# A third pair of token chunks by Strassen's products in an attention and feed-forward kernel, with sums and small scalings moved between engines

## The chip, the cores and the metric

The kernel runs on one core of a Trainium2 chip. The core has TensorE for matrix products (PE in the profile, with PEld for its weight loads), VectorE (DVE), ScalarE (ACT), GpSimd (POOL) and SyncE (SP), whose queue issues nearly all DMA transfers here. The metric is the device time of one execution in microseconds, the median of several executions.

## The reference, cut to what matters

```python
# attention over pooled keys, q, k, v: [8 batches, 8 heads, 576 tokens, 64]
k_p = k.reshape(B, H, 72, 8, D).mean(axis=3)
v_p = v.reshape(B, H, 72, 8, D).mean(axis=3)
scores = scale * np.matmul(q, k_p.transpose(0, 1, 3, 2))
scores = scores - np.max(scores, axis=-1, keepdims=True)
attn = np.exp(scores)
attn = attn / (np.sum(attn, axis=-1, keepdims=True) + 1e-09)
x = np.matmul(attn, v_p)            # then [4608 tokens, 512]
# feed-forward, w1, w2: [512, 1024], w3: [1024, 1024], w_out: [1024, 512]
a = x @ w1
b = x @ w2
out = ((a * b) @ w3) @ w_out
```

## The kernel before

The 4608 tokens are 12 chunks of 384 columns. `w3 @ w_out` is formed once at the start (`w_mm`, L1048), as eight blocks `W[j]`. Every large product is made of three TensorE passes over a high and a low part of each operand (`PASSES`), in float32r.

**A plain chunk** m (`range(NP)`, L1363) has eight units j. A unit is twelve matmuls of 384 columns for a (`a_mm`), twelve for b (`b_mm`), both at L785, and nine matmuls of 512 columns that add `(a*b)` times `W[j]` to three PSUM accumulators (`out_mm`, L817, L833). Between them ScalarE copies a (`a_post`), VectorE multiplies (`b_post`), ScalarE rounds to the high part (`g_hi`, L810) and VectorE subtracts for the low part (`g_lo`, L815).

**A pair** M takes two chunks at once (L1392): per unit, seven block products of six matmuls of 384 columns each (`prod`, L951, L962) replace the 48 matmuls that the two chunks would need for a and b. The inputs are sums and differences of blocks of x (`x_sum1` to `x_plo`, tiles `X`) and of the weights (`mix`, L878, written to DRAM as `ws` and read back through a ring of eleven tiles of 256 KB, `load_u`, L942). The results of the products meet in PSUM banks a, b and c: `s1_copy`, `s5_copy`, `s2_copy` on ScalarE, `c11`, `c12`, `c22`, `g_first`, `g_second` on VectorE. The seventh product adds to bank a, and so needs `c22` (L987) to have read what the sixth left there; the sixth needs `s2_copy` (L976) likewise. The out products of the pair's first chunk are spread between the products of the next unit (`out_some`, L848), so that most units have some of them ahead of the seventh product; those of its second chunk follow the eight units (`out_mm` again). Before the change `NP` is 8: chunks 0 to 7 are plain, and chunks 8 and 9, 10 and 11 are pairs 4 and 5.

**Attention** for later chunks runs between these products: scores on TensorE (`s_mm`, L533), softmax on VectorE and ScalarE (`soft1` to `soft2`), transposes by VectorE and through DRAM (`te_turn`, `te_out`, `te_in`), and the product with v (`av_mm`, L737). K and V are summed over groups of eight either by one VectorE reduction (`pool_red`, L467) or by three adds on GpSimd (`pool_tree`, L470). `SOFT_ACT` names the tiles of tokens whose exponentials also give the sums on ScalarE, tile by tile of heads.

**The order of work** on every engine is one list. Each function is put into it with a slot number by `at(kind, k, fn, ...)` (three slots to a unit of a plain chunk), the number is corrected by hand in a table `SHIFT`, and the list is sorted. `M0` is the slot at which chunk 0 begins, `M1 = M0 + 24*NP` that of the first pair. The same list sets the order of SP's queue, which works in order: a transfer that waits for its buffer holds up all behind it.

Of the kernel before, what the change touches and what calls it, by code (L numbers as in the profile page):

```python
# [19 lines left out]
def kernel(  # L20
# [40 lines left out]
    SOFT_ACT = [(0, 0), (0, 1), (1, 0), (1, 1), (1, 2), (1, 3), (2, 1), (2, 2), (3, 1), (3, 2), (4, 1), (4, 2),  # L61
        (4, 3), (5, 0), (5, 1), (5, 2), (6, 0), (6, 1), (6, 2), (7, 1), (7, 3), (8, 1), (8, 2), (9, 1), (9, 2),
        (10, 1), (10, 2), (10, 3), (11, 1), (11, 2)]
    HALF = [(0, 2), (2, 0), (3, 0), (4, 0), (5, 0), (6, 0), (7, 0), (8, 0), (9, 0), (10, 0), (10, 2), (11, 0)]
# [997 lines left out]
    def W_lo(i):  # L1062
# [10 lines left out]
        "g_first": {(4, 6): 0.5, (5, 6): 0.5},
        "g_hi": {(0, 0): 0.75, (0, 1): 0.5, (0, 2): 0.25, (0, 4): 0.5, (0, 6): 0.5, (10, 0): -0.25, (10, 3):
            -0.5, (2, 3): 0.75, (9, 0): 0.5},
        "g_lo": {(0, 0): 0.25, (0, 1): 0.75, (0, 2): 2.5, (0, 4): 0.25, (0, 7): 1.75, (10, 0): 0.75, (10,
# [11 lines left out]
        "load_k": {(0, 0): 3.25, (0, 2): 1},  # L1088
        "load_q": {(11, (3,)): -0.25, (5, (3,)): 0.75, (7, (3,)): 0.75, (9, (3,)): 0.75},
        "load_qt": {(0, 0): -0.5, (0, 1): -0.25, (0, 2): 2},  # L1090
        "load_v": {(0, 0): -0.75, (0, 1): -2},
# [3 lines left out]
            -22.75, (3,): -31, (4,): -10, (5,): -22, (8,): -0.25},  # L1095
        "load_wo": {(0,): -44, (1,): -30, (2,): -5},
        "mix": {(7, 0): -0.75},
        "mix_hi": {(3, 1): 0.5, (5, 0): -0.5, (5, 1): -0.5, (7, 0): -0.5, (7, 1): -0.5},
        "mix_lo": {(3, 1): 0.5, (6, 0): 0.75, (6, 1): 0.75},
        "mix_load": {(1, 0): -0.25},  # L1100
        "mix_out": {(5, 0): 1, (5, 1): 1},
        "plain_out": {(5, 1): 0.75, (7, 1): 0.75},
        "prep_k": {(0, 0): 3.5, (0, 1): 1.25, (1, 0): 0.5, (1, 1): 0.5, (1, 2): -0.75},
        "prep_v": {(1, 1): 5.25},
# [386 lines left out]
```

## Time and profile before

| | |
|---|---|
| median of 3 runs | 743.82 us (743.68 to 746.69) |
| profiled execution, device time | 744.73 us |
| its span, first to last instruction | 742.8 us |
| outside its span | 1.93 us |
| PE busy | 730.5 us, 98% |
| DVE, ACT, POOL busy | 469.8, 352.8, 174.9 us |

The span is the part of the profiled execution that the trace shows; the 1.93 us before and after it belong to the time as well. Busy times are unions of an engine's instructions. Durations of single matmuls overlap, so a matmul's cost is read from the distance between starts.

### The profile page before, as it was taken

The page shows a single profiled execution, that of the slowest core. Times are in us where ns is not written, and L with a number is a line of the kernel's source. Part 1 is how long each engine was busy: PE and PEld are TensorE (multiplying, and loading weights), DVE is VectorE, ACT ScalarE, POOL GpSimd, SP SyncE. Part 2 cuts the span into 40 slices and gives each one's busy share as a digit, 9 for nine tenths or more (in the row PEclk, how much of TensorE's full clock was granted, in tenths as well). Part 3 has the DMA queues.
Part 4 walks back from the last instruction along what each step waited for, and adds up shares of the span by engine and source line. Part 5 has one row for each costly group of instructions (what it writes and reads, how often), then busy time and mean ns, then how long its engine had stood idle before and what let it go on. Part 6 is the DMA issues. An engine that isn't in the chain of part 4 may idle for free.

```text
span 742.8 us, 12190 instructions
## 1 busy us (share of the span) xinstructions
PE 730.5 (98%) x4088; PEld 681.1 (92%) x4088; DVE 469.8 (63%) x875; ACT 352.8 (47%) x1059; POOL 174.9 (24%) x228
## 2 busy tenths in 40 slices
PE   7999999999999999999999999999999999999997
PEld 6888999999999999999999999999989999899996
DVE  4788877665675845664658658566885586633342
ACT  6888986442442634434433434353454344422222
POOL 2244384033431531004503312033042000000000
PEclk9999999999999999999999999999999999999999
DMA  8989935187386465486656463826498859176611
GB/s 288 360 258 307 310 125 125 49 227 191 106 212 155 147 161 153 129 198 181 176 125 185 130 169 97 175 81 155 115 333 241 237 169 301 64 211 197 198 56 42
DMA packets 177741, 132.60 MB, mean 179 GB/s; under 512 B 78352, under 2 KB 145104, under 8 KB 177680
## 3 DMA queue, kind: packets, MB, share of 16 engines
q1 hardware_dynamic: 177536, 131.70, 62.4%
q8 instruction: 32, 0.52, 0.3%
q14 instruction: 29, 0.24, 0.1%
q10 hardware_dynamic: 144, 0.13, 0.1%
HBM read 94.63 MB, written 37.16 MB: 177 GB/s over the span
## 4 chain that ended last, share of the span: by engine, by line
PE 95%; DMA 3%; DVE 1%; SPq 0%; issue 0%; ACT 0%; DVEq 0%; ACTq 0%
PE o L833 22%; PE a L785 18%; PE b L785 18%; PE a L962 8%; PE att L533 5%; PE att L737 5%; PE o L1054 4%; PE o L848 4%; PE att L962 4%; PE b L962 2%; DMA raw<-in_moe_w_dram 1%; PE b L1054 1%; PE a L1054 1%; DMA D<-T 1%; DMA PTl<-D 1%; PE att L238 1%
## 5 line engine op out<-in xcount | busy, mean ns | idle before, releaser
L833 PE MATMUL o<-Wc,gh 128*128 128x512 f32 (+1 forms) x480 | 149.3, 392 | 0.0
L785 PE MATMUL b<-xT,hl 128*128 128x384 f32 x768 | 145.7, 339 | 0.0
L785 PE MATMUL a<-xT,hl 128*128 128x384 f32 x768 | 145.6, 338 | 0.0
L785 PEld LDWEIGHTS a<-xT,hl 128*128 128x128 f32 x768 | 133.4, 188 | 2.9
L785 PEld LDWEIGHTS b<-xT,hl 128*128 128x128 f32 x768 | 132.8, 188 | 0.0
L810 ACT CAST gh<-a 128x384 fp32r<-128x384 f32 x80 | 41.0, 513 | 126.5 <-DVE a L805 103.3
L833 PEld LDWEIGHTS o<-Wc,gh 128*128 128x128 f32 x480 | 87.4, 188 | 13.9 <-DVE ob L863 0.2
L833 PE MATMUL o<-Wc,gl 128*128 128x512 f32 (+1 forms) x240 | 93.1, 388 | 0.2 <-DVE gl L815 0.2
L571 ACT ACTIVATE E<-att,mx 128x72 f32<-128x72 f32 (+1 forms) x240 | 73.5, 324 | 28.2 <-DVE mx L549 26.5
L962 PE MATMUL a<-X,ring 128*128 128x384 f32 x384 | 77.6, 337 | 2.7 <-DVE tmp L987 1.7
L962 PEld LDWEIGHTS a<-X,ring 128*128 128x128 f32 x384 | 67.7, 188 | 6.5 <-DVE tmp L987 2.3
L805 DVE TENSOR_TENSOR a<-b,a 128x384 f32<-128x384 f32 x64 | 35.1, 549 | 50.3 <-PE b L785 48.5
L795 ACT COPY a<-a 128x384 f32<-128x384 f32 x64 | 30.8, 482 | 73.6 <-PE a L785 73.4
L471 POOL TENSOR_TENSOR st<-st 128x512 f32<-128x512 f32 (+2 forms) x29 | 38.6, 1333 | 113.0 <-DMA st<-in_v_dram 63.2
L833 PEld LDWEIGHTS o<-Wc,gl 128*128 128x128 f32 x240 | 45.0, 188 | 10.6 <-DVE gl L815 1.1
L815 DVE TENSOR_TENSOR gl<-a,gh 128x384 fp32r<-128x384 f32 x80 | 47.1, 589 | 6.9 <-ACT gh L810 6.5
L882 POOL TENSOR_TENSOR mix<-mix 128x256 f32<-128x256 f32 x16 | 13.1, 819 | 161.2 <-DMA mix<-wr 132.1
L571 ACT ACTIVATION_READ_ACCUMULATOR E<-att,mx 128x1 f32 (+1 forms) x240 | 50.1, 209 | 0.0
L533 PE MATMUL att<-kbd,qT 128*128 128x144 f32 (+1 forms) x320 | 49.9, 286 | 0.0
L533 PEld LDWEIGHTS att<-kbd,qT 128*128 128x128 f32 (+1 forms) x320 | 45.8, 179 | 1.7
L549 DVE TENSOR_REDUCE mx<-att 128x4 f32<-128x288 f32 (+1 forms) x80 | 35.3, 446 | 16.3 <-PE att L533 16.1
L1054 PE MATMUL o<-hl 128*128 128x512 f32 x144 | 38.8, 401 | 0.0
(158 smaller groups left out, 1167.7 us busy)
## 6 DMA issues: line engine op xcount, KB each, us to landing
ring<-ws SPq DMA_DIRECT2D x112, 256.0 KB
raw<-in_moe_w_dram SPq DMA_DIRECT2D x32, 512.0 KB
out_dram<-ob SPq DMA_DIRECT2D x35, 256.0 KB
st<-in_v_dram SPq DMA_DIRECT2D x16, 512.0 KB
ws<-mix SPq DMA_DIRECT2D x32, 256.0 KB
st<-in_k_dram SPq DMA_DIRECT2D x24, 288.0 KB
qs<-in_q_dram SPq DMA_DIRECT2D x112, 48.0 KB
D<-T SPq DMA_DIRECT2D x7, 768.0 KB
```

The costliest lines, as they stand in the source:

```text
L471: eng.tensor_tensor(out=t[:, :, 0:4], in0=t[:, :, 0:4], in1=t[:, :, 4:8], op=ALU.add)
L533: nc.tensor.matmul(out=ps[:nt, 2 * KP * j:2 * KP * (j + 1)], lhsT=qT[n][:, pr, off:off + nt], rhs=kbd[b % 2][:, pr], start=True, stop=True,)
L549: nc.vector.tensor_reduce(out=mx[:nt, hs], in_=sv, axis=AX.X, op=ALU.min)
L571: nc.scalar.activation(out=E[:nt, h], in_=sv[:, i], func=AF.Exp, scale=-1.0, bias=mx[:nt, h:h + 1], accum_out=sm[:nt, h:h + 1])
L737: nc.tensor.matmul(out=Tp[n, pr, "x"][:, off:off + cnt], lhsT=parts[x][0], rhs=parts[x][1], start=x == 0, stop=x == 3)
L785: nc.tensor.matmul(out=o, lhsT=w12[j, w][sw][:, kt * P:(kt + 1) * P], rhs=x[sx][:, kt], start=(i == 0), stop=(i == 3 * NK - 1))
L805: nc.vector.tensor_tensor(out=g, in0=ps[:, :CH], in1=g, op=ALU.mult)
L810: nc.scalar.copy(out=gh, in_=g)
L815: eng.tensor_tensor(out=gl, in0=g, in1=f(gh), op=ALU.subtract)
L833: nc.tensor.matmul(out=o, lhsT=(gh, gl)[sg][:, c], rhs=W[j][sw][:, d], start=(j == 0 and i == 0), stop=(j == NJ - 1 and i == 2))
L962: nc.tensor.matmul(out=o, lhsT=w[:, kt, sw], rhs=x[sx][:, kt], start=first and n == 0, stop=n == 5, skip_group_check=True)
L1054: nc.tensor.matmul(out=wacc[h][it], lhsT=w3t[s][sa][:, it * P:(it + 1) * P], rhs=wo[j][sb], start=(j == 0 and i == 0), stop=(j == NJ - 1 a ...
```

## The change

`NP` goes from 8 to 6: chunks 6 and 7 become pair 3. K and V sums on VectorE are made by the three adds instead of one reduction, and 16 of them (14 of K, 2 of V) instead of 19 are on VectorE; five of the sixteen weight mixes go from GpSimd to VectorE. For the 29 tiles in `SOFT_ACT` (30 before) the sum is scaled on ScalarE. The last unit's out product of the chunk or pair ahead of a pair is put later, so that it stands between the pair's sixth and seventh product, and the copies of that chunk's result go with it. The mixes and the plain parts of the weights are written to DRAM earlier; q of chunk 7 is staged in two of the four K/V staging tiles; many slot numbers change.

```diff
-    NP = 8
+    NP = 6
...
-    MIX_DVE = []
+    MIX_DVE = [(2, 0), (2, 1), (5, 1), (7, 0), (7, 1)]
...
-    K_RED = [(2, 2), (2, 3), (3, 1), (3, 2), (3, 3), (4, 0), (4, 1), (4, 2), (4, 3), (5, 1), (5, 2), (5, 3), (6,
-        1), (6, 3), (7, 1), (7, 2), (7, 3)]
-    V_RED = [(5, 0), (5, 1)]
+    K_RED = [(2, 2), (2, 3), (3, 1), (3, 2), (3, 3), (4, 1), (4, 2), (5, 0), (5, 1), (5, 3), (6, 0), (6, 2), (7,
+        1), (7, 2)]
+    V_RED = [(3, 0), (7, 1)]
...
     def q_stage(n, pr):
-        if False:
+        if n == NP + 1:
             if pr % 2 == 0:
                 stage["q", n, pr // 2] = st_tile([P, 2 * CH])
...
             if (b, i) in K_RED:
-                pool_red(t[:KP], km[b][:KP, i])
+                pool_tree(t[:KP], km[b][:KP, i], nc.vector)
...
-    def pool_red(t, dst):
-        nc.vector.tensor_reduce(out=dst, in_=t.rearrange("k a e d -> k a d e"), axis=AX.X, op=ALU.add)
-
...
-        (pool_red if (b, hf) in V_RED else pool_tree)(stage.pop(("v", b, hf)), vm[b][:, 2 * hf:2 * hf + 2])
+        eng = nc.vector if (b, hf) in V_RED else nc.gpsimd
+        pool_tree(stage.pop(("v", b, hf)), vm[b][:, 2 * hf:2 * hf + 2], eng)
...
-        nc.vector.tensor_scalar(
-            out=sm[:nt], in0=sm[:nt], scalar1=1e-9, scalar2=float(POOL), op0=ALU.add, op1=ALU.mult)
+        if (n, t) in SOFT_ACT:
+            nc.scalar.activation(out=sm[:nt], in_=sm[:nt], func=AF.Copy, scale=float(POOL), bias=POOL * 1e-9)
+        else:
+            nc.vector.tensor_scalar(
+                out=sm[:nt], in0=sm[:nt], scalar1=1e-9, scalar2=float(POOL), op0=ALU.add, op1=ALU.mult)
...
-            at("M", k + 5, out_mm, m, j)
+            at("M", k + 5 + 1.2 * ((m, j) == (NP - 1, NJ - 1)), out_mm, m, j)
         for t in range(3):
-            at("P", m0 + 3 * NJ + 3, out_post, m, t)
+            at("P", m0 + 3 * NJ + 3 + 2 * (m == NP - 1), out_post, m, t)
...
-        k = M0 + 30 + 24 * (u // 3) + 6 * (u % 3)
+        k = M0 + 6 + 24 * ((u + 2) // 4) + 5 * ((u + 2) % 4)
...
-        at("L", M0 + PLAIN + 8 * u, plain_out, j, kt)
+        at("L", M0 + PLAIN + 6 * u, plain_out, j, kt)
...
-            at("M", k + 1 + j, out_mm, 2 * M + 1, j)
+            at("M", k + 1 + j + 3.2 * (j == NJ - 1 and M < NCH // 2 - 1), out_mm, 2 * M + 1, j)
         if M < NCH // 2 - 1:
             for t in range(3):
-                at("P", k + 1 + NJ, out_post, 2 * M + 1, t)
+                at("P", k + 5 + NJ, out_post, 2 * M + 1, t)
...
+        if n == NP + 1:
+            k = BASE[n] = k - 3
...
-                k2 = x + 2 + 2 * kt
+                k2 = x + 2 - (n == NP + 1) + 2 * kt
...
-            plan_q(n, *((k - 3.25, 0.5, k - 1.5, 0.5) if n == NP + 1 else (k - 8, 1, k - 4, 1)))
+            plan_q(n, *((k - 9, 0.5, k - 4.5, 0.5) if n == NP + 1 else (k - 8, 1, k - 4, 1)))
...
-            plan_v(b, k + 1, k + 3, k + 6, k + 9, k + 10)
+            plan_v(b, *(k + x - 8 * (b == 4) for x in (1, 3, 6, 9, 10)))
```

The rest of the diff is new entries of the lists `SOFT_ACT` and `HALF` and of `SHIFT`: `c11` one slot later in nearly every unit of a pair, `load_u` one slot later in all, `g_lo` mostly later, and the first loads of `w3` (3 and 4) and `w_out` (0) earlier.

## Rows read from the trace of the kernel before

**Rows 1.** The page: engines' busy time, share of the span and instructions.

```profile
PE 730.5 (98%) x4088; PEld 681.1 (92%) x4088; DVE 469.8 (63%) x875; ACT 352.8 (47%) x1059; POOL 174.9 (24%) x228
```

**Rows 2.** Stretches: start, plain chunks, pair 4, pair 5; busy times, clock, DMA.

```profile
0.00:76.60 76.60, 71.15 (x395) 60.50 (x396) 56.91 (x109) 62.48 (x147) 27.66 (x39) 1.00 0.97 306
76.60:536.80 460.20, 460.02 (x2604) 434.85 (x2603) 303.29 (x557) 218.12 (x711) 134.38 (x174) 1.00 0.58 153
536.80:645.90 109.10, 107.17 (x590) 99.50 (x589) 76.53 (x151) 49.85 (x157) 12.82 (x16) 1.00 0.74 224
645.90:742.80 96.90, 92.19 (x505) 86.28 (x503) 33.09 (x60) 22.36 (x45) 0.00 (x0) 0.99 0.48 147
```

**Rows 3.** PE's waits before 76.6 us for weights: us in total, times, longest.

```profile
PE att L238 <- DVE Wc L186: 1.4, 1, 1.4
...
PE att L236 <- DVE Wc L186: 0.9, 1, 0.9
```

**Rows 4.** Timeline of PE in a plain unit: start, length, work.

```profile
504.16 2.24 PE L785 MATMUL b<-xT,hl 128*128 128x384 f32 x12
506.24 0.62 PE L833 MATMUL o<-Wc,gh 128*128 128x512 f32 x2
...
508.29 2.24 PE L785 MATMUL a<-xT,hl 128*128 128x384 f32 x12
```

**Rows 5.** Timeline of PE in pair 5: two products in a row.

```profile
646.98 1.20 PE L962 MATMUL a<-X,ring 128*128 128x384 f32 x6
648.02 1.20 PE L962 MATMUL att<-X,ring 128*128 128x384 f32 x6
```

**Rows 6.** Timeline of PE: a sixth product, then its three waits inside the pairs.

```profile
545.72 1.31 PE L962 MATMUL a<-X,ring 128*128 128x384 f32 x6
547.98 1.31 PE L962 MATMUL a<-X,ring 128*128 128x384 f32 x6 [0.95 <-DVE tmp L987]
...
576.71 1.31 PE L962 MATMUL a<-X,ring 128*128 128x384 f32 x6 [0.96 <-ACT tmp L976]
...
653.08 1.31 PE L962 MATMUL a<-X,ring 128*128 128x384 f32 x6 [0.74 <-DVE tmp L987]
```

**Rows 7.** Groups by form, whole span: sums of K by reduction, adds of these sizes.

```profile
L468 DVE TENSOR_REDUCE km<-st 72x128 f32<-72x1024 f32 x17 | 34.0, 1998 | 0.6 <-DMA st<-in_k_dram 0.5
...
L418 DVE TENSOR_TENSOR st<-st 128x512 f32<-128x512 f32 x2 | 1.4, 693 | 0.9 <-DMA st<-in_k_dram 0.9
...
L422 DVE TENSOR_TENSOR km<-st 64x128 f32<-64x128 f32 x4 | 1.1, 287 | 0.2
...
L419 DVE TENSOR_TENSOR st<-st 128x256 f32<-128x256 f32 x2 | 0.8, 425 | 0.1
```

**Rows 8.** Source line of the scaled sum: nanoseconds least, median, most.

```profile
L591 DVE TENSOR_SCALAR sm<-sm x40: 124/168/1277, 52.0 to 609.1; 128x8 f32<-128x8 f32 x24, 96x8 f32<-96x8 f32 x16
```

**Rows 9.** Source line of g_lo in pair 4, then pair 5: nanoseconds.

```profile
L815 DVE TENSOR_TENSOR gl<-a,gh x9: 544/558/1396, 536.8 to 622.6; 128x384 fp32r<-128x384 f32 x9
...
L815 DVE TENSOR_TENSOR gl<-a,gh x8: 558/558/559, 653.2 to 717.7; 128x384 fp32r<-128x384 f32 x8
```

**Rows 10.** Timeline at pair 4's start: VectorE, then GpSimd.

```profile
548.04 1.40 DVE L815 TENSOR_TENSOR gl<-a,gh 128x384 fp32r<-128x384 f32 x1
...
546.31 0.74 POOL L472 TENSOR_TENSOR st<-st 128x256 f32<-128x256 f32 x1
547.12 0.65 POOL L473 TENSOR_TENSOR vm<-st 128x128 f32<-128x128 f32 x1
547.74 1.28 POOL L471 TENSOR_TENSOR st<-st 128x512 f32<-128x512 f32 x1
```

**Rows 11.** What SP's queue waited for in pair 4: the longest.

```profile
SPq L866 <- ACT ob L865: 16.6, 1, 16.6
```

**Rows 12.** The page: DMA issues by kind, count and size.

```profile
ring<-ws SPq DMA_DIRECT2D x112, 256.0 KB
...
st<-in_k_dram SPq DMA_DIRECT2D x24, 288.0 KB
```

More of the change, by code (lines that the diff above doesn't have):

```diff
@@ L59 @@
     SLOTS, SLOTS1 = 11, 3
[L61 to L64, printed above, removed]
+    SOFT_ACT = [(0, 0), (0, 1), (1, 0), (1, 1), (1, 2), (1, 3), (2, 1), (2, 2), (3, 1), (3, 2), (4, 1), (5, 0),
+        (5, 2), (6, 0), (6, 1), (6, 2), (7, 0), (7, 1), (7, 2), (7, 3), (8, 1), (8, 2), (9, 1), (9, 2), (10, 1),
+        (10, 2), (10, 3), (11, 1), (11, 2)]
+    HALF = [(0, 2), (2, 0), (3, 0), (4, 0), (5, 1), (5, 2), (6, 0), (7, 0), (7, 3), (8, 0), (9, 0), (10, 0),
+        (10, 2), (11, 0)]
     LO12_POOL = [(0, 1), (2, 1), (3, 0), (3, 1), (4, 0), (4, 1), (5, 1), (7, 1)]
@@ L1068 @@
         "W_lo": {(1,): 0.25, (2,): 0.5, (3,): 12, (5,): 2.25, (6,): 2.25, (7,): 2.75},
+        "a_post": {(5, 0): 0.25, (5, 1): 0.25, (5, 2): 0.25, (5, 3): 0.25, (5, 4): 0.25, (5, 5): 0.25, (5,
+            6): 0.25, (5, 7): 0.25},
         "av_lo": {(0, 0): 0.25, (0, 1): 0.75, (0, 2): 0.75, (0, 3): 1, (1, 0): 0.5, (8, 3): 3.5},
-        "av_mm": {(0, 3): 0.5, (1, 0): 0.5, (8, 3): 3.75},
+        "av_mm": {(0, 3): 0.5, (1, 0): 0.5, (11, 2): -1, (5, 2): -1, (7, 2): -1, (8, 3): 3.75, (9, 2): -1},
         "av_post": {(0, 0): 0.25, (0, 3): 0.5, (1, 0): 0.5, (8, 3): 3},
         "b_post": {(0, 4): 0.25},
[L1073 to L1076, printed above, removed]
[7 rows of a table removed]
[4 rows of a table added]
+        "g_first": {(3, 0): 0.25, (3, 2): 0.5, (3, 6): 0.5, (4, 0): 0.25, (4, 6): 0.5, (5, 6): 0.5},
+        "g_hi": {(0, 0): 0.75, (0, 1): 0.5, (0, 2): 0.25, (0, 4): 0.5, (0, 6): 0.5, (10, 1): 0.25, (10, 2):
[7 rows of a table added]
+        "g_lo": {(0, 0): 0.25, (0, 1): 0.75, (0, 2): 2.5, (0, 4): 0.25, (0, 7): 1.75, (10, 0): 1.25, (10,
[12 rows of a table added]
         "kr_mm": {(0,): -0.25, (1,): 2.5},
@@ L1087 @@
         "kt_post": {(0,): -1.25, (1,): 3.5},
-        "load_k": {(0, 0): 3.25, (0, 2): 1},
-        "load_q": {(11, (3,)): -0.25, (5, (3,)): 0.75, (7, (3,)): 0.75, (9, (3,)): 0.75},
-        "load_qt": {(0, 0): -0.5, (0, 1): -0.25, (0, 2): 2},
-        "load_v": {(0, 0): -0.75, (0, 1): -2},
+        "load_k": {(0, 0): 3.25, (0, 2): 1, (3, 3): -3, (4, 3): -1.5, (6, 3): -1.5, (7, 1): -0.5, (7, 2):
+            -4},
+        "load_q": {(10, (0,)): -0.75, (10, (1,)): 1.75, (10, (2,)): 1.75, (10, (3,)): 1.75, (11, (3,)):
+            -0.25, (4, (0,)): 3, (4, (1,)): 2.5, (4, (2,)): 2.5, (4, (3,)): 2.5, (5, (3,)): 0.75, (6, (0,)):
+            2, (6, (1,)): 1.5, (6, (2,)): 1.5, (6, (3,)): 1.5, (8, (0,)): 1.5, (8, (1,)): 1, (8, (2,)): 1,
+            (8, (3,)): 1, (9, (3,)): 0.75},
+        "load_qt": {(0, 0): -0.5, (0, 1): -0.25, (0, 2): 2},
+        "load_u": {(3, 0, 0): 1, (3, 0, 1): 1, (3, 0, 2): 1, (3, 0, 3): 1, (3, 0, 4): 1, (3, 0, 5): 1, (3,
[24 rows of a table added]
+        "load_v": {(0, 0): -0.75, (0, 1): -2, (3, 0): -0.25, (3, 1): -0.25, (4, 0): -2, (4, 1): -2, (6, 0):
+            -2, (6, 1): -2},
         "load_vr": {(0,): -3},
@@ L1094 @@
         "load_w3": {(0,): -59, (1,): -35, (10,): -0.25, (11,): -0.75, (13,): -1.5, (15,): 2.75, (2,):
[L1095 to L1104, printed above, removed]
+            -22.75, (3,): -33.75, (4,): -20.25, (5,): -22, (8,): -0.25},
+        "load_wo": {(0,): -44.5, (1,): -30, (2,): -5},
+        "mix": {(2, 1): -1.75, (7, 0): -0.25, (7, 1): 0.5},
+        "mix_hi": {(0, 1): -0.75, (4, 0): -1.25, (4, 1): -0.75, (5, 0): -0.5, (5, 1): -0.5, (6, 0): -1.25,
+            (6, 1): -0.75, (7, 0): -0.5, (7, 1): -0.5},
+        "mix_lo": {(3, 1): 0.5, (4, 0): 0.25, (4, 1): 0.25, (5, 1): 0.5, (6, 0): -0.5, (6, 1): 0.75, (7, 1):
+            0.5},
+        "mix_out": {(4, 0): -0.25, (4, 1): -0.25, (5, 0): 1, (5, 1): 0.25, (6, 0): -0.25, (6, 1): -0.25},
+        "out_post": {(1, 1): 2.5, (3, 2): 1, (5, 0): -0.5, (5, 1): -1, (5, 2): -0.5, (7, 1): 2.5, (9, 0):
+            0.5, (9, 1): -0.5},
+        "plain_out": {(4, 1): 1.5, (5, 0): -3, (5, 1): -2.25, (6, 0): 1.5, (6, 1): 1.5, (7, 0): -3, (7, 1):
+            -2.25},
+        "prep_k": {(0, 0): 3.5, (0, 1): 1.25, (1, 0): 0.5, (1, 1): 0.5, (1, 2): -0.75, (3, 1): 1.5, (5, 3):
+            1.25, (6, 1): 0.5, (7, 1): 0.5, (7, 2): -2.5, (7, 3): -0.5},
+        "prep_v": {(1, 1): 5.25, (4, 0): -1, (5, 1): 1, (6, 1): 0.75},
         "prep_v2": {(0, 1): 0.5},
@@ L1161 @@
             2.5, (6, 0): 2.5, (6, 1): 2.5, (7, 0): 2.25, (7, 1): 4.5},
[L1162 to L1174 removed]
+        "te_in": {(10, 0): 0.75, (10, 1): 2, (11, 0): 0.25, (3, 0): 1, (4, 0): 1.5, (5, 0): 1.75, (6, 0):
+            0.25, (7, 0): 0.25, (7, 1): 0.25, (8, 0): 0.75, (9, 0): 0.25},
+        "te_out": {(10, 0): 0.25, (10, 1): 0.25, (11, 0): -0.25, (3, 0): -1, (4, 0): 0.25, (4, 1): 0.25, (5,
+            0): -1.25, (8, 0): -0.75, (9, 0): -1},
+        "te_post": {(10, 1): 1.25, (11, 0): 1.5, (11, 1): 2.25, (3, 0): 1, (3, 1): 1, (4, 0): 0.5, (4, 1):
+            1.25, (5, 0): 1, (5, 1): 0.75, (6, 0): 0.75, (6, 1): 0.5, (8, 0): 1.5, (8, 1): 1.25, (9, 0):
+            1.5, (9, 1): 1.25},
+        "te_rest": {(10,): 1.5, (11,): 0.75, (5,): 0.5, (8,): 1.25, (9,): 0.75},
+        "te_turn": {(10, 0): 0.25, (10, 1): 0.25, (10, 2): 1.75, (10, 3): 0.25, (11, 0): -0.25, (11, 1):
[3 rows of a table added]
+        "tr_q": {(10, 0): 0.75, (10, 3): 0.5, (7, 0): 1.25, (7, 1): 1.25, (7, 2): 1.25, (7, 3): 1.25, (8,
+            1): 1, (8, 3): -3, (9, 0): 0.5, (9, 1): 0.5, (9, 2): 0.5, (9, 3): 0.5},
         "vr_hi": {(0,): -0.25},
```

28 lines of the change are left out of this document (7 added, 21 removed), and 102 rows, old and new, of the table SHIFT.

## The prediction

> **What bounds the kernel now.** I read the page's engine line first: PE is busy for 730.5 of 742.8 us [rows 1]. A mean can hide stages with other limits, so the stretches come next. In the plain chunks PE is busy for 460.02 of 460.20 us, in pair 4 for 107.17 of 109.10, and the clock is 1.00, the 2.4 GHz level, in both [rows 2]; what is lost outside them lies in the start, the last pair and its tail. So nearly everywhere the time is the number of matmuls times their pace, and the other engines matter only where they make PE wait. PE's list of waits and its timeline give those places: two waits for weights before 76.6 us, 1.4 and 0.9 us [rows 3], and three in the pairs, each in front of a product that adds to bank a: 0.95 and 0.74 us for `c22` in the first unit of pairs 4 and 5, and 0.96 us for `s2_copy` later in pair 4 [rows 6]. Together the last three are 2.65 us. A busy PE need not run at its best pace, so the timeline also gives the pace. Twelve matmuls of 384 columns take 506.24 − 504.16 = 2.08 us, 0.173 us each, and nine of 512 columns take 508.29 − 506.24 = 2.05 us [rows 4]; a pair's product of six takes 648.02 − 646.98 = 1.04 us, again 0.173 each [rows 5]. The pace is the same in either form, so counting instructions is enough.
>
> **The third pair.** Two plain chunks issue 2 × 8 × 24 = 384 matmuls of 384 columns for a and b, a pair 8 × 7 × 6 = 336. The out products, 144 in either form, the attention and the start stay. PE is rid of 48 × 0.173 = 8.3 us, and since PE has no slack in plain chunks or pairs, all of it is on the path.
>
> **The moved out product.** It is nine matmuls, 2.05 us [rows 4]. In the first unit of a pair there is no `out_some` yet, so after the sixth product nothing covers the copy or sum that the seventh waits for. Moved in front of the seventh, the 2.05 us are longer than either wait for `c22`, 0.95 and 0.74 us [rows 6]: both go, −1.7 us. The new pair 3 would have brought a third and doesn't. What is late next: the sixth product now comes 1.04 us after the fourth, as it does in pair 5's first unit, where PE did not wait there. The three copies of the earlier chunk's result then start about two products, 2.1 us, later and hold the accumulators that the next unit's `out_some` needs; by the slot numbers that comes 6.8 − 3.2 = 3.6 slots of 1.9 us (five to a unit of 9.3 us, below) after the product begins, 4.7 us after it ends; I cost that at nothing, and at up to 1 us in each of three pairs if VectorE or ScalarE is full there.
>
> **The attention that pair 3 now carries.** Pair 4, with attention of two chunks in it, had one wait of 0.96 us for ScalarE; pair 5, with none, had no such wait. Two pairs now carry attention, so I add one more, +1.0 us; bounds 0 (both gone) and 1.9 (pair 3 like pair 4 with both its kinds of wait).
>
> **Sums on VectorE.** The trace has 19 reductions at 2.0 us [rows 7], 38 us. The 16 that stay become three adds of 512, 256 and 128 elements: 0.69 + 0.43 + 0.29 = 1.4 us by the rows of such adds on full height [rows 7], 22.5 us in all. Three more sums on GpSimd cost it 1.28 + 0.74 + 0.65 = 2.7 us each [rows 10], 8 us; five mixes leave it. The five on VectorE are one add of 256 elements and two of 128, 0.43 + 2 × 0.29 = 1.0 us each, 5 us. So the sums make VectorE about 10 us lighter if its adds run undisturbed; pair 3 itself costs it seven instructions a unit in place of four, 24 × 0.56 us [rows 9] = 13 us, in a stretch that by pair 4's row is busy 76.53 of 109.10 us [rows 2]. None of that is on the path: VectorE is busy 303.29 of 460.20 us there, GpSimd 134.38 [rows 2]. If this cover went, the worst is a VectorE instruction held by one of GpSimd's: 63 two-input instructions (48 adds, 15 of the mixes) × at most 1.28 us [rows 10] = 81 us more of VectorE, within its 157 us of idle time in the plain stretch, though not within the idle time next to each one. I take nothing for the path.
>
> **Scaling on ScalarE.** It takes 29 small instructions from VectorE, whose median is 0.17 us but whose longest is 1.28 us [rows 8], and puts as many on ScalarE, which is busy 218.12 of 460.20 us [rows 2]. Nothing of it on the path; the bounds are −1.0 us (should the remaining wait for ScalarE or VectorE vanish) and +1.0 (one more such wait).
>
> **Transfers.** A pair reads 56 ring tiles of 256 KB [rows 12], 14.7 MB more, and the mixes are squeezed from eight chunks into six. In pair 4 the DMA engines were busy 0.74 at 224 GB/s [rows 2], so full would be near 300 GB/s. Pair 3 lies earlier in the attention than pair 4 did, so by the slot numbers it also holds two batches of K, eight loads of 288 KB [rows 12], and q of one more chunk, 0.8 MB: 3.2 MB, 10 us, or 0.84 of 108 us. SP works in order, but the ring holds eleven tiles, eleven products: 11/7 of a unit of 7 × 1.04 + 2.05 = 9.3 us, so 14.7 us of cover. I take nothing; the price of losing the cover is a rival below. The earlier weight loads at the start, where the DMA engines are busy 0.97 [rows 2], can win at most the 2.3 us of waits there [rows 3] or lose as much; I take nothing.
>
> **The sum.** 742.8 − 8.3 − 1.7 + 1.0 = 733.8 us of span; with 1.93 outside it 735.7 against the profiled execution's 744.73, that is −9.0. The median of the runs, 743.82, lies 0.9 below that execution, so I predict **734.8 us**. The likeliest case's own range is 730.6 to 738.7: 743.8 − 8.3 with all three pair waits gone and 2.3 won at the start, against −8.3 with pair 3 adding 1.9, both old `c22` waits gone by 1.7 and three late accumulators costing 3.0.
>
> **Rivals.**
>
> *VectorE is held up by GpSimd, and gives part of the gain back.* Pair 4's first unit shows it: the subtraction `g_lo` that takes 558 ns at the median took 1.40 us at 548.04, while GpSimd's add ran from 547.74 to 549.02; in pair 5, where GpSimd does nothing [rows 2], eight of them lie between 558 and 559 ns [rows 9, 10]. The Trainium skill, SBUF — State Buffer, section Who interferes with whom, says that a VectorE instruction with two SBUF inputs and a GpSimd instruction that reads SBUF shut each other out for a whole instruction, and that a reduction never contends; by that rule the change swaps 19 immune instructions for 48 that can be held, and the trace agrees that such holding happens. By the rule at its worst the sum keeps its value only as long as none of the 63 holds falls just ahead of a product; by the plain stretch's row none does. Against it: in the plain stretch, with GpSimd busy for 134 us, PE lost 0.2 us, since the next unit's products cover one hold. It decides where two holds of 1.28 us fall into the 2.05 us of cover ahead of a seventh product. Pair 3 has GpSimd sums of K in it besides those that pair 4 had. With four waits of 0.95 us in pairs 3 and 4 together beyond my sum, 734.8 + 3.8 = 738.6.
>
> *SP's queue runs the ring dry: slower.* A K or V load in pair 3 waits at the head of the queue for one of the four staging tiles, two of which q of chunk 7 now takes for a time, and every ring tile waits behind it. Pair 4 had a head that waited 16.6 us for a ScalarE copy [rows 11], harmless because the ring was full and 16 us of out products followed. In the middle of a pair, what goes beyond 14.7 us stops PE. To end slower by over 0.5% it must cost 9.0 + 3.7 = 12.7 us, a wait of 27.4 us, to 747.5. For it: eight K loads and four more of V and q stand among the ring's. Against it: no PE wait for a transfer stands in the pairs now. A wait of 24 us would leave 744, no change.
>
> *The start of pair 3 comes before its inputs.* Chunk 7's attention has four tiles of tokens where chunk 9's had three, and all sums of x hang on its last product with v. Pair 4's first product followed without a gap. If they are late by one slot, 2.4 us (a plain unit and its attention take 460.2/64 = 7.2 us for three slots [rows 2]), the time is 737.2.
>
> **How the numbers follow.** No change means within 0.5%, 740.1 to 747.5, about what a measurement of this kernel can tell. I give the sum 0.62, GpSimd's holds 0.16, late inputs 0.10, the dry ring 0.12, of which 0.05 slower. Most of the first three end below 740.1: faster 0.86, same 0.09, slower 0.05. The range must hold eight in ten; from the bounds of the sum and the two smaller rivals I take 731.5 to 739.5, which leaves out the dry ring and the ends of the start's gain and of the holds.
>
> **What would show it.** Right: 336 × 3 = 1008 matmuls at L962's place, 576 each for a and b, PE busy near 722 us, no wait over 0.3 us in front of a seventh product of a first unit, the sums of K and V on VectorE near 22.5 us. Wrong: PE waits that name a ring transfer (the dry ring), `c22` or `g_lo` in later units beside long two-input adds (holds), or X tiles ahead of pair 3's first products (late inputs). A PE busy time that falls by much more or less than 8.3 us would break the count itself.

## The result, and the profile after

The changed kernel takes **755.35 us** (median of 6 runs, 748.50 to 758.29) where the kernel before took 743.70 beside it (743.64 to 746.69). It is slower, by 11.7 us from median to median; the ratio taken over all these runs is 1.0133, 95% interval 1.0087 to 1.0178, which is 9.9 us. Forecast was 734.8, so the forecast missed by 20.55 us, and its range ended at 739.5. The runs also lie much further apart than those of before. The profiled execution took 751.39 us with a span of 749.3, one of the quicker ones, so the profile shows 6.5 us of the loss and not all of it.

First the page of the changed kernel: the engine line that answers to [rows 1], the chain's shares by engine, and the ring's issues that answer to [rows 12].

```profile
PE 730.4 (97%) x4040; PEld 676.4 (90%) x4040; DVE 479.9 (64%) x929; ACT 360.0 (48%) x1089; POOL 178.6 (24%) x222
...
PE 76%; DMA 9%; SPq 6%; DVE 5%; issue 2%; ACT 2%; DVEq 0%; ACTq 0%
...
ring<-ws SPq DMA_DIRECT2D x168, 256.0 KB
```

The chain's shares in the kernel before were

```profile
PE 95%; DMA 3%; DVE 1%; SPq 0%; issue 0%; ACT 0%; DVEq 0%; ACTq 0%
```

The 48 matmuls are gone (4088 to 4040), yet PE's busy time did not fall with them: 730.4 us. The chain that ended last now runs for 15% through transfers and SP's queue, where it was 3%. Where this happens is seen in windows of both kernels; the columns are length, then busy time (instructions) of PE, PEld, VectorE, ScalarE and GpSimd, granted clock, DMA share, GB/s. Before:

```profile
80.00:300.00 220.00, 220.00 (x1263) 208.20 (x1263) 143.80 (x271) 112.34 (x384) 75.92 (x93) 1.00 0.57 156
300.00:440.00 140.00, 139.82 (x777) 131.76 (x776) 89.93 (x159) 58.74 (x189) 34.16 (x47) 1.00 0.63 163
440.00:540.00 100.00, 100.00 (x564) 94.72 (x563) 69.78 (x128) 44.46 (x135) 22.01 (x30) 1.00 0.51 131
```

After:

```profile
80.00:300.00 220.00, 218.95 (x1254) 206.09 (x1253) 149.71 (x299) 113.31 (x373) 80.30 (x96) 1.00 0.64 177
300.00:440.00 140.00, 136.46 (x753) 127.76 (x752) 87.18 (x172) 61.91 (x213) 34.56 (x43) 0.99 0.59 158
440.00:540.00 100.00, 95.77 (x510) 88.00 (x509) 71.29 (x133) 45.63 (x142) 23.09 (x28) 0.98 0.88 246
```

PE was idle for 0.18 us of these 460; now it is idle for 1.05, 3.54 and 4.23 us, 8.8 in all, most of it in the last plain chunks and in pair 3. The clock dips where it waits.

Idle time is not the whole loss. From the first product of chunk 0 to that of pair 4 the kernel before took 460.2 us [rows 2]; the changed one takes 468.0 (76.40 to 544.40) with 8.3 us of matmuls less. So 16.1 us are lost there, and 8.8 of them are idle. The rest lies in busy time: at a lower clock matmuls are slow without being idle, and a wait costs more than its idle time. In [rows 6] two products start 2.26 us apart where six matmuls take 1.04, so 1.22 us are lost, of which the profile calls 0.95 idle.

The list of PE's waits names the places (us in total, times, longest):

```profile
PE a L964 <- ACT a L970: 3.0, 1, 3.0
PE att L739 <- ACT E L570: 1.6, 1, 1.6
...
PE a L964 <- DVE tmp L989: 1.3, 1, 1.3
...
PE att L430 <- DVE km L471: 0.9, 1, 0.9
```

None of them names a transfer. The chain in pair 3 says what stands behind the longest (start, length, work):

```profile
452.70 5.65 DMA D<-T
...
459.72 8.77 DMA PTl<-D
...
468.58 0.06 ACT PTh L705
...
470.05 0.48 ACT a L970
470.57 2.29 PE a L964 x6
```

`te_out` writes chunk 8's turned scores to DRAM and `te_in` reads them back; the data are there at 468.5. ScalarE works in order: `te_post`'s split (L705) waits for them, `s1_copy` (L970) stands behind it, and PE wants bank a. So a late transfer stops PE under ScalarE's name, and the next product's six matmuls take 2.29 us, against 1.20 for six in [rows 5], at a clock that the profile puts at 0.81 for 466 to 475 us, below the 2.4 GHz level. In the kernel before, the same chunk's round trip ran beside plain chunks, 9.65 us from the write's issue to the first split; the two rows of its timeline:

```profile
461.80 0.36 SPq L667 DMA_DIRECT2D D<-T  x1
...
471.45 0.83 ACT L703 CAST PTh<-PTl 128x768 fp32r<-128x768 f32 x1 [1.01 <-DMA PTl<-D]
```

In the changed kernel it takes 468.58 − 452.70 = 15.9 us. The DMA share is 1.00 during these 15.9 us and was 0.75 during those 9.65. The second place is the end of the plain chunks:

```profile
340.82 16.29 SPq L359 DMA_DIRECT2D st<-in_q_dram  x32
...
360.20 0.43 SPq L669 DMA_DIRECT2D D<-T  x1
...
369.80 1.57 ACT L705 CAST PTh<-PTl 128x768 fp32r<-128x768 f32 x2 [1.81 <-DMA PTl<-D]
```

SP spends 16.3 us on issuing the 32 loads of chunk 7's q, 0.51 us each, and only then comes to what is behind them. VectorE has turned chunk 6's scores by 357.48; they leave at 360.20 and are split from 369.80 on. VectorE's three subtractions for them stand ahead of maxima of other scores, ScalarE's exponentials come behind the maxima, and PE's attention product at 376.93 waits 1.6 us for those. One of the subtractions (L701) takes 2.08 us where their median is 0.95; a sum on GpSimd begins beside it at 372.97. Lateness alone does not explain this wait. In the kernel before, the same chunk's round trip was longer and ended later:

```profile
361.81 0.34 SPq L667 DMA_DIRECT2D D<-T  x1
...
373.98 1.57 ACT L703 CAST PTh<-PTl 128x768 fp32r<-128x768 f32 x2 [3.00 <-DMA PTl<-D]
```

ScalarE waited 3.0 us for it and PE lost nothing; no maximum and no exponential stood behind that split before 384 us. So the trip's time and the changed order make this wait together; in the experiments an earlier trip (wide q) and a later split each take it away.

Three shorter waits of PE, at 337.6, 345.7 and 353.8 us, 1.9 us together, name VectorE's `g_lo` and a sum of K. The chain to the first of them goes through SP's queue too, by another way:

```profile
329.12 0.40 SPq L391 DMA_DIRECT2D st<-in_k_dram  x1
...
334.23 0.69 DVE L469 TENSOR_TENSOR st<-st 72x512 f32<-72x512 f32 x1 [2.52 <-DMA st<-in_k_dram]
```

A load of K goes out behind 16 loads of q, VectorE waits 2.5 us for it, and its adds, a weight mix and `g_lo` follow in order.

### The profile page after: what moved, and what is told of

Same layout as the page of the kernel before. It is cut to its first block, busy times and chain, and to the rows that moved or that the text cites. A ratio compares the mean times of both kernels' runs of the same rounds, so it can differ in the third digit from the quotient of the medians.

```text
span 749.3 us, 12300 instructions
## 1 busy us (share of the span) xinstructions
PE 730.4 (97%) x4040; PEld 676.4 (90%) x4040; DVE 479.9 (64%) x929; ACT 360.0 (48%) x1089; POOL 178.6 (24%) x222
## 4 chain that ended last, share of the span: by engine, by line
PE 76%; DMA 9%; SPq 6%; DVE 5%; issue 2%; ACT 2%; DVEq 0%; ACTq 0%
PE o L835 15%; PE a L964 11%; PE a L787 10%; PE b L787 10%; PE att L964 6%; PE o L850 5%; PE o L1056 4%; PE att L532 4%; PE att L739 4%; DMA PTl<-D 4%; SPq L359 3%; PE b L964 3%; DMA D<-T 1%; DMA raw<-in_moe_w_dram 1%; PE b L1056 1%
## 5 line engine op out<-in xcount | busy, mean ns | idle before, releaser
L835 PE MATMUL o<-Wc,gh 128*128 128x512 f32 (+1 forms) x432 | 135.0, 394 | 0.6 <-DVE ob L865 0.6
L964 PE MATMUL a<-X,ring 128*128 128x384 f32 x576 | 117.6, 339 | 4.7 <-ACT a L970 3.0
L964 PEld LDWEIGHTS a<-X,ring 128*128 128x128 f32 x576 | 102.7, 189 | 10.2 <-ACT a L970 3.4
L787 PE MATMUL b<-xT,hl 128*128 128x384 f32 x576 | 109.5, 339 | 0.0
L787 PE MATMUL a<-xT,hl 128*128 128x384 f32 x576 | 109.2, 338 | 0.0
L787 PEld LDWEIGHTS a<-xT,hl 128*128 128x128 f32 x576 | 100.0, 188 | 2.3
L787 PEld LDWEIGHTS b<-xT,hl 128*128 128x128 f32 x576 | 99.4, 188 | 0.1
L964 PE MATMUL att<-X,ring 128*128 128x384 f32 x288 | 58.8, 340 | 0.5 <-ACT tmp L975 0.5
L964 PEld LDWEIGHTS att<-X,ring 128*128 128x128 f32 x288 | 50.4, 189 | 1.1 <-ACT tmp L975 1.1
L850 PE MATMUL o<-Wc,gh 128*128 128x512 f32 x144 | 48.4, 394 | 0.0
```

The lines of the kernel that those rows point to most:

```text
L787: nc.tensor.matmul(out=o, lhsT=w12[j, w][sw][:, kt * P:(kt + 1) * P], rhs=x[sx][:, kt], start=(i == 0), stop=(i == 3 * NK - 1))
L835: nc.tensor.matmul(out=o, lhsT=(gh, gl)[sg][:, c], rhs=W[j][sw][:, d], start=(j == 0 and i == 0), stop=(j == NJ - 1 and i == 2))
L850: nc.tensor.matmul(out=oacc[m][t], lhsT=(gh, gl)[sg][:, t * P:(t + 1) * P], rhs=W[j][sw], start=(j == 0 and i == 0), stop=(j == NJ - 1 and ...
L964: nc.tensor.matmul(out=o, lhsT=w[:, kt, sw], rhs=x[sx][:, kt], start=first and n == 0, stop=n == 5, skip_group_check=True)
```

## The experiments

All ratios are to runs of the kernel before on the same chip, and the profiles are of one execution each. A difference is called shown where the intervals lie apart; sizes in us are differences of the ratios times 743.8, and the changed kernel's own interval leaves each of them open by some 3 us.

**K sums and q: two edits that did not help.** First q of chunk 7 from GpSimd's queue:

```diff
-                        nc.sync.dma_start(
+                        (nc.gpsimd if n == NP + 1 else nc.sync).dma_start(
```

> The changed kernel with one thing moved: the 32 loads of chunk 7's q go out from GpSimd's queue, not SP's. In the changed kernel they hold SP for 16.3 us (340.8 to 357.1) ahead of the write of chunk 6's turned scores. Theory Q (SP issues one transfer in 0.45 us, in order, and its backlog makes the attention's way through DRAM late): that write goes out some 3 us earlier or more, PE's wait of 1.6 us near 377 and the low clock behind it go, 3 to 6 us off 755, about 750. Theory T (the DMA engines are overfull with ring tiles and mixes, whoever issues): within 1 us of the changed kernel. Theory V (VectorE's adds are late or held): no gain either, or a loss, as GpSimd gets more to do.

761.20 us, 1.0231 (1.0211 to 1.0251): worse. Its waits:

```profile
PE o L835 <- DVE gl L817: 5.8, 4, 4.4
PE a L964 <- ACT a L970: 3.6, 1, 3.6
PE att L430 <- POOL km L471: 3.4, 1, 3.4
```

GpSimd issues in order too: its first 16 issues took 341.86 to 350.99, and a sum of K began behind them at 351.87. The Trainium skill, DMA: Bandwidth & Descriptors, section Rules for kernel authors, says that spreading transfers over the issuing engines saves only sequencer time; here it moved that time to an engine that PE also waits for. Then the sums by reduction again, as in the kernel before:

```diff
-                pool_tree(t[:KP], km[b][:KP, i], nc.vector)
+                pool_red(t[:KP], km[b][:KP, i])
```

> The changed kernel with the K and V sums that stand on VectorE made by one reduction again instead of three adds; the same tiles, the same places in the order. Theory V (the adds are held by GpSimd, or stand in VectorE's way): 5 us or more off 755, with g_lo's longest instruction shorter. Theories Q and T: within 2 us of the changed kernel, or up to 2 us slower, since a reduction takes 2.0 us where three adds take 1.4.

752.63 us, 1.0119 (1.0073 to 1.0165): not told apart from the changed kernel, and the 3.0 us wait stays. The two intervals leave room for a gain of some 5 us, so this run does not exclude a smaller cost of the adds.

**The other parts by themselves.** The moved product alone, on the kernel before:

```diff
-            at("M", k + 5, out_mm, m, j)
+            at("M", k + 5 + 1.2 * ((m, j) == (NP - 1, NJ - 1)), out_mm, m, j)
-            at("M", k + 1 + j, out_mm, 2 * M + 1, j)
+            at("M", k + 1 + j + 3.2 * (j == NJ - 1 and M < NCH // 2 - 1), out_mm, 2 * M + 1, j)
```

> The kernel before, with two plain-paired chunks as it had (eight plain chunks), and only the last out product ahead of each pair, with the copies behind it, put between the sixth and seventh product. By the prediction's step: PE's waits of 0.95 and 0.74 us go, 1.7 us off 743.7, 742.0. Rival: the copies of the earlier result come late for the next unit's out products, and half or all of it is lost: 743 to 744.

743.64 us, 0.9991 (0.9970 to 1.0012); its profiled span is 740.9, 1.9 below that of before, with the `c22` wait of pair 5 gone and 0.58 us left of that of pair 4. The runs can't confirm a gain of that size. The scaling back on VectorE in the changed kernel:

```diff
-        if (n, t) in SOFT_ACT:
+        if False:
```

> The changed kernel with the softmax sums scaled on VectorE again in every tile (no scaling on ScalarE): the last part of the change that no run has undone. If this part costs what the prediction took, nothing: 752 to 757 us. If it costs time through ScalarE's order or through VectorE's wait for ScalarE: 748 to 751 us.

750.79 us, 1.0098 (1.0079 to 1.0116). It lies where a cost through order was expected, but the intervals overlap, so a cost of this part is neither shown nor excluded. The VectorE mixes back on GpSimd (`MIX_DVE = []`), and the 32 plain weight writes on GpSimd's queue (`nc.gpsimd.dma_start` in `plain_out`):

> The changed kernel with the five weight mixes that went to VectorE back on GpSimd, at the same places in the order. Theory D: VectorE no longer stands between a late load of K and the queue of SP, which waits for the mix's buffer: the waits of 0.5 us for g_lo and the one for the sum of K go, 2 to 4 us off 755. Theories S and R: within 1.5 us of 755.

> The changed kernel with the 32 writes of the plain weights issued from GpSimd's queue in place of SP's: the same bytes, 32 transfers fewer for SP. If SP's time per transfer is what is short ahead of pair 3 (0.45 to 1.4 us each, some 20 us), 2 to 5 us off 755; if the DMA engines' time is, or VectorE's order, no gain, or a loss where sums on GpSimd come late behind the issues.

751.50 us, 1.0116 (1.0089 to 1.0143), and 751.86 us, 1.0111 (1.0094 to 1.0129): neither is told apart from the changed kernel.

**Bytes.** Ring tiles by half in all three pairs:

```diff
-        nc.sync.dma_start(out=f(t), in_=ws[j][:, WSLOT[ORDER[i][0]]])
+        nc.sync.dma_start(out=f(t[:, 0]), in_=ws[j][:, WSLOT[ORDER[i][0]], 0])
-                nc.tensor.matmul(out=o, lhsT=w[:, kt, sw], rhs=x[sx][:, kt],
+                nc.tensor.matmul(out=o, lhsT=w[:, 0, sw], rhs=x[sx][:, kt],
```

> The changed kernel with each of the 168 ring tiles read only by half (128 KB): the weights' second half of the inner dimension is left out and the first is used twice. The number of transfers, of matmuls and their order stay. Theory T: the waits of pairs 3 and 4 for attention data (3.0 us at 470, 1.3 at 586, the clock behind them) go, 5 to 8 us off 755, while what is lost ahead of pair 3 (some 6 us) stays: 747 to 750. Theory Q: SP issues as many transfers as before, so not more than 2 us off. Theory V: none off.

745.95 us, 1.0030 (1.0013 to 1.0048): shown, some 7.7 us. The same in the kernel before, as control:

> The kernel before with its ring tiles (pairs 4 and 5) read by half. If transfers are late only through the third pair: no change, 742.5 to 744.5 us. If the pairs of the kernel before already lose time to their transfers, and the gain of halving the ring in the changed kernel says nothing of the change: 737 to 741 us.

743.97 us, 0.9996 (0.9981 to 1.0011): nothing. Only pair 3 by half (the edit above under `if M == 3`):

> The changed kernel with the ring tiles of pair 3 alone read by half (128 KB in place of 256 KB; the other half of each product takes the same weights twice), those of pairs 4 and 5 whole. Theory 'third pair' (the lost time lies where the new pair's reads meet the transfers of attention, K, V and q): most of what halving all three gave, 746 to 749 us, and the 3.0 us wait near 470 shrinks. Rival (pairs 4 and 5 lose as much): 751 to 755 us.

748.99 us, 1.0061 (1.0039 to 1.0082): shown, about 5.4 of the 7.7. The weight writes taken out (`mix_out` and `plain_out` issue nothing, the ring reads the first copies `wr`), with whole and with half tiles:

> The changed kernel without the 64 transfers that write the mixed and plain weights to DRAM (12.6 MB); the mixes are still computed, and the ring tiles are read, as many and as large, from the unmixed weights, so the products are others. Theory S (squeezing these writes from eight chunks into six is what makes the attention's transfers late ahead of pair 3): the 6 us lost between 320 and 385 go, 748 to 749, and the waits inside the pairs stay. Theory R (the ring's traffic does it): what is lost in the plain stretch stays, 754 to 755. Theory D (VectorE, in whose order mixes and sums of late K now stand, passes the lateness on): half of it, 751 to 753.

> The run before with the ring tiles read by half as well. If late transfers, of weights and ring together, are the whole cause of the lost gain, this comes near the sum of the prediction, 735 to 738. If something else takes part (the order on VectorE and ScalarE, GpSimd's holds), 740 or more, with PE waits left that name VectorE or ScalarE behind no transfer.

753.71 us, 1.0134 (1.0105 to 1.0162), and 742.88 us, 0.9986 (0.9972 to 0.9999). With whole tiles, taking the writes out gains nothing that shows; with half tiles it is worth 1.0030 to 0.9986, 3.3 us, and the intervals lie apart. The profile of the first suggests why whole tiles hide it: from 320 to 385 us PE is idle for 1.33 us in place of 3.54, but from 440 to 540 for 6.90 in place of 4.23, so in this execution the loss moved into pair 3. With half tiles and no writes the time is level with before, and still 5 to 8 us above the 735 to 738 expected if late transfers were the whole cause.

**SP's queue.** q of chunks 2 to 11 in 256-byte rows, half of the issues, the same bytes (their order in the tile is then another, so the scores are those of a shuffled q):

```diff
-                    for db in range(2):
-                        g = 2 * par + db
...
-                            out=t[32 * g:32 * g + 32, off // 32:(off + cnt) // 32],
+                        out=t[64 * par:64 * par + 64, off // 64:(off + cnt) // 64],
```

> The changed kernel with q of chunks 2 to 11 loaded in 256-byte rows to 64 partitions, two transfers a head pair and piece in place of four with 128-byte rows: the same bytes, half of the issues on SP and half of the packets. The elements of q stand in another order in the tile, so the scores are those of a shuffled q. Theory 'queue' (SP's own time for issuing the 32 loads of chunk 7, 16.3 us, and the small packets hold back the round trip of the turned scores): SP's stretch of chunk 7's loads halves to about 8 us, 745 to 750 us. Theory 'bytes' (the third pair's ring reads fill the engines): 752 to 756 us.

748.71 us, 1.0051 (1.0028 to 1.0074): shown, about 6.1 us. The Trainium skill, DMA: Bandwidth & Descriptors, section Rules for kernel authors, advises to coalesce many small transfers into larger ones; by that rule the run should gain, and it did. SP's stretch of issues for chunk 7 is 11.2 us in place of 16.3, and chunk 6's scores leave at 354.27 in place of 360.20. Of these 5.9 us, 3.2 come from VectorE, which turns them at 353.57 in place of 356.81, because the load of K goes out earlier and VectorE waits less for it:

```profile
326.26 0.40 SPq L388 DMA_DIRECT2D st<-in_k_dram  x1
...
330.73 0.69 DVE L466 TENSOR_TENSOR st<-st 72x512 f32<-72x512 f32 x1 [0.67 <-DMA st<-in_k_dram]
```

The control:

> The kernel before with q of chunks 2 to 11 loaded in 256-byte rows and half of the issues (q shuffled). If the queue's time costs something only with the third pair beside it: 742.5 to 744.5 us. If the kernel before pays for it too: 737 to 741 us, and the 7 us in the changed kernel say little of the change.

743.99 us, 0.9991 (0.9973 to 1.0008): the kernel before does not pay for it.

**Order.** The same instructions, `te_post` of chunks 6 and 8 about one step later (the entries that change, cut from their tables):

```diff
 "te_post":
-    (6, 0): 0.75, (6, 1): 0.5, (8, 0): 1.5, (8, 1): 1.25
+    (6, 0): 1.75, (6, 1): 1.5, (8, 0): 2.25, (8, 1): 2.0
 "te_rest":
-    (8,): 1.25
+    (6,): 0.75, (8,): 1.75
```

> The changed kernel with the splits of the turned scores placed one step later in two attentions: those of chunk 8 behind the copy of the second product in pair 3's fourth unit, those of chunk 6 behind that unit's VectorE add and ScalarE cast. The same instructions, only their order on ScalarE and VectorE. Theory 'order' (a late transfer costs TensorE time because the copies that wait for it stand in order ahead of work that TensorE wants): TensorE's waits of 3.0 us behind the copy of bank a (near 470) and of 1.6 us behind the exponentials (near 377) go, with the slower clock after them; 747 to 751 us against 755.4. Theory 'data' (the turned scores themselves come too late): the waits only move to the attention products that read the turned scores (their line then names ScalarE's split), and the time stays within 753 to 757.

749.43 us, 1.0071 (1.0045 to 1.0097); the interval overlaps that of the change, and the next run, which holds the same edit, lies clear of it:

> The order edit of the run before it (splits of chunks 6 and 8 later) and more of the kind: the second split of chunk 10 behind the sum that frees bank a in pair 4, the turn of one batch's pooled K one step later, the first three attention products of chunk 8 one step later. Nothing but order changes. Theory 'order': each of the waits near 353 (0.9 us), 467 (1.8 and 0.7 us) and 583 (1.4 us) goes or shrinks, 745 to 748 us against 749.4. If the waits only move on: 748.5 to 751 us.

747.61 us, 1.0049 (1.0028 to 1.0070). The edits are further entries in `SHIFT`: `te_post` (10, 1) from 1.25 to 2.25, `kt_mm` and `kt_post` of batch 5 one later, `av_mm`, `av_post` and `av_lo` of chunk 8's first three products one later. But a wait in its profile (its slowest execution, 752.0 us) shows the limit of reordering:

```profile
PE att L964 <- ACT tmp L975: 4.6, 2, 4.1
```

With the split one place later, `s5_copy` (L975) stood behind it in place of `s1_copy`: as long as the data come late, the next copy in the queue takes the wait. Both GpSimd edits on top:

> The same order edits, and the five VectorE sums of weight blocks back on GpSimd, and the 32 plain writes of weight blocks issued on GpSimd's queue. A version that could beat both kernels: with each part's gain (order 6 us, the two others 1 to 4 each where the intervals allow) 741 to 746 us; if they do not add, 746 to 750 us.

748.53 us, 1.0043 (1.0018 to 1.0067): nothing more that shows. No version that keeps all of the work is shown to be faster than the kernel before.

**One loss or several.** Splits later, q wide and pair 3 by half together:

> Three edits of single runs together: the splits of chunks 6 and 8 later, q in 256-byte rows with half of the issues, ring tiles of pair 3 by half (with that, q shuffled and pair 3's products fed with half of their weights). Each alone gave 6 to 7 us. If they are three separate losses: 736 to 739 us, the time that the prediction gave the change without a late transfer. If all three are the one lateness of the same round trips, seen from three sides: 743 to 747 us.

743.09 us, 0.9995 (0.9973 to 1.0017). The single gains of q (0.82%) and bytes (0.72%) add to 1.54%, and the three together gave 1.38%; the order edit alone gave 0.62% (0.84% with its additions). So q and bytes look like two losses, and the order edit like another treatment of the same two. The ratios alone can't tell this, since each is open by some 0.3%; windows over the two places, 320 to 385 and 440 to 480 us, columns as above, support it. The change:

```profile
320.00:385.00 65.00, 61.46 (x334) 56.52 (x333) 41.59 (x87) 31.25 (x131) 18.97 (x22) 0.97 0.56 145
440.00:480.00 40.00, 36.91 (x195) 34.67 (x194) 24.54 (x45) 15.96 (x55) 5.04 (x6) 0.96 0.93 246
```

q wide:

```profile
320.00:385.00 65.00, 65.00 (x368) 61.01 (x369) 43.71 (x92) 36.46 (x155) 19.54 (x24) 1.00 0.56 161
440.00:480.00 40.00, 36.83 (x196) 35.00 (x195) 22.16 (x39) 13.44 (x38) 5.17 (x6) 0.96 1.04 261
```

Splits later (the first order edit):

```profile
320.00:385.00 65.00, 62.56 (x352) 58.36 (x351) 39.98 (x86) 33.99 (x143) 19.34 (x22) 1.00 0.59 156
440.00:480.00 40.00, 37.48 (x199) 35.44 (x198) 22.84 (x43) 14.29 (x51) 5.05 (x6) 0.96 0.99 245
```

Pair 3 by half:

```profile
320.00:385.00 65.00, 61.86 (x343) 56.53 (x342) 42.61 (x87) 31.43 (x131) 18.95 (x22) 1.00 0.57 147
440.00:480.00 40.00, 38.23 (x212) 36.13 (x211) 26.05 (x47) 16.08 (x56) 5.55 (x6) 1.00 0.80 190
```

All three together:

```profile
320.00:385.00 65.00, 64.72 (x364) 60.35 (x363) 43.62 (x91) 36.03 (x155) 20.46 (x23) 1.00 0.56 161
440.00:480.00 40.00, 39.03 (x215) 36.68 (x213) 26.05 (x44) 14.89 (x43) 6.86 (x8) 1.00 0.81 210
```

Wider q takes away all 3.5 us of PE's idle time in the first place and none in the second; fewer bytes take 1.3 us in the second and 0.4 in the first; later splits take 1.1 in the first and 0.6 in the second; together both places shrink, and the clock stays at 1.00.

**The rest.** All transfer remedies and the later splits at once:

> The changed kernel with every transfer remedy at once and the later splits: no writes of weight blocks, all ring tiles by half and read from the first copies, q in 256-byte rows with half of the issues, the splits of chunks 6 and 8 later (pairs are fed with wrong weights, q is shuffled). If the rest above 736 us is still transfers: 735 to 739 us. If it is the third pair's own order of work on ScalarE and VectorE under attention: it stays at 741 to 744 us, with TensorE's waits naming those two engines.

741.81 us, 0.9986 (0.9970 to 1.0001), no less than with the writes gone and half tiles. Its profiled span is 739.3 us. The first products of pairs 3 and 4 in its timeline:

```profile
428.29 1.31 PE L955 MATMUL b<-X,ring 128*128 128x384 f32 x6
...
536.33 1.22 PE L955 MATMUL b<-X,ring 128*128 128x384 f32 x6
```

It begins its plain chunks at 76.21, so chunks 0 to 7 take 460.1 us, as in the kernel before (460.2, [rows 2]), though they hold 8.3 us less of matmuls. Its waits there are small and many:

```profile
PE att L736 <- DVE PTl L704: 1.3, 2, 0.8
...
PE att L736 <- DMA ring<-wr: 0.7, 1, 0.7
PE o L832 <- DVE ob L862: 0.6, 1, 0.6
PE att L955 <- ACT tmp L966: 0.5, 1, 0.5
PE o L847 <- DVE gl L814: 0.5, 1, 0.5
```

All but one name VectorE or ScalarE, which is the sign that was expected of the pair's own order of work. But a late transfer shows under the same names, as above, and at least three of these waits are of that kind. PE waits 1.5 us in all at 319.17, 320.42 and 321.40, behind splits that waited for a round trip. SP sent its write at 301.56, then stood for 4.9 us at the load of V next in its queue, which waited for a staging tile that a GpSimd sum of K had to free, and only then, at 308.80, issued the reading back:

```profile
SPq L455 <- POOL km L468: 4.9, 1, 4.9
...
317.07 0.83 ACT L702 CAST PTh<-PTl 128x768 fp32r<-128x768 f32 x1 [3.23 <-DMA PTl<-D]
...
320.42 0.45 PE L736 MATMUL att<-PTl,vbd 128*128 128x384 f32 x1 [0.80 <-DVE PTl L704]
```

Another, 0.55 us at 371.74, comes behind two subtractions of VectorE (L704) that take 3.33 us where the same two take 1.83 in the changed kernel (370.66), beside sums on GpSimd. So what is left over is not one thing.

## Why the prediction was wrong

**The step that failed: "Transfers … I take nothing".** It asked whether the ring would run dry, found 14.7 us of cover, and was right about that: the list of PE's waits in the changed kernel names no ring tile. The traffic was sized well too: the step worked out a DMA share of 0.84 for pair 3, and it is 0.87 (432.80 to 544.40 us). What failed is the step from there to nothing. It did not ask what else stands on the same queue and engines. Attention's round trip has no ring in front of it, and in pair 3 it takes 15.9 us, at a DMA share of 1.00, in place of the 9.65 that it took beside plain chunks. At the end of the plain chunks SP's time for issuing q holds back a load of K and the round trip of chunk 6. By the runs, halving q's issues gave back about 6.1 us and halving the bytes of pair 3's ring about 5.4, neither of which the kernel before pays. Since a longer trip of chunk 6 cost the kernel before nothing, the new order of work has a part in the first of these. Among its signs of being wrong the prediction had only "PE waits that name a ring transfer" for transfers: a late transfer showed as a wait for ScalarE or VectorE.

**The attention that pair 3 carries: too small, and its cause is open in part.** The step took +1.0, with bounds 0 and 1.9. In the kernel with everything relieved, chunks 0 to 7 still take 460.1 us, where the sum gave 460.2 − 8.3 + 1.0 = 452.9. So some 7 us come back without the transfers that were taken out. PE is idle for 4.9 of them: 2.25 us in pair 3, just beyond the bound of 1.9, and 2.66 in the six plain chunks, where the steps on sums and scaling took nothing; the rest lies in busy time. At least 1.5 us of the latter stand behind a round trip that SP's queue held, so these are transfers again; which of the edits to VectorE's and ScalarE's work bring the others stays open. Reductions in place of adds and scaling on VectorE each gave a lower median, and neither interval is apart from the change's.

**The count: right.** There are 1008 matmuls at L964 and 576 each for a and b, 48 fewer. The forecast "PE busy near 722" failed, since busy time takes in part of each wait and the slower matmuls at the lower clock. So PE's busy time was no test of the count; the instructions are.

**The moved product: right, as far as shown.** No first unit's seventh product waits over 0.1 us in the changed kernel, and alone it took 1.9 us off the profiled span; the runs bound it to between −2.2 and +0.9 us. The price was taken from idle time, 0.95 us, where the distance between starts gives 1.22, so by the same rows each such wait was priced some 0.27 us too low.

**Sums on VectorE: mis-sized; whether they cost time stays open.** Their groups in the changed kernel:

```profile
L469 DVE TENSOR_TENSOR st<-st 72x512 f32<-72x512 f32 x14 | 10.1, 723 | 2.5 <-DMA st<-in_k_dram 2.5
L470 DVE TENSOR_TENSOR st<-st 72x256 f32<-72x256 f32 x14 | 8.6, 614 | 0.5
L471 DVE TENSOR_TENSOR km<-st 72x128 f32<-72x128 f32 x14 | 6.3, 447 | 0.6
```

That is 25 us for K, 1.78 a sum against the 1.4 of [rows 7], and with V's two about 30 in place of 22.5. VectorE is 10 us busier in all where the step made it lighter by 10 and pair 3 heavier by 13. The step set VectorE's idle time as a whole against them, though it noted itself that not all of that lies next to the instructions that need it. PE's 1.9 us of waits for `g_lo` and a sum of K stand behind adds and a mix on VectorE, which had begun late for want of a load.

**The rivals.** Holds by GpSimd were priced at +3.8; a kernel without these adds is not told apart from the change, and edits to transfers and order bring the time level with the kernel before, so holds are not the main cause. They occur all the same: instructions of VectorE that take well over their usual time beside GpSimd's stand ahead of the 1.6 us wait at 376.93 and of a wait in the relieved kernel. Late inputs of pair 3 did not show. The dry ring had the right sign and the right place, SP's queue and the DMA engines, and the wrong victim; a load that waits for a staging tile did hold the queue, with the round trip behind it. At 0.05 for slower it was priced by the deepest cover on that queue and not by the shallowest.

## What to carry to other kernels

Before a transfer is costed at nothing, list everything that shares its queue and its DMA engines, and price the one with the least slack, not the one that was added: here a round trip through DRAM with nothing ahead of it, behind 32 small loads. A late transfer shows up under the name of the engine whose in-order queue waits for it, so for each PE wait that names a copy, look at what that copy stood behind. An edit that only reorders can help, as far as other work fits ahead of the wait (here 0.84%, shown); in an execution where the data came later still, the wait moved to the next copy. And read a wait's cost from the distance between starts, not from idle time alone.
